# Ten result slots a head, gates on GpSimd and measured spacings in the attention; disjoint scatter views and another order in the experts

## The chip, the core and the metric

The kernel runs on one core of a Trainium2 chip. The metric is the time of one execution on the device in microseconds (us), the median of several runs. The engines are named as the profile does: PE (TensorE, matrix products; PEld are its weight loads), DVE (VectorE), ACT (ScalarE), POOL (GpSimd) and SP (SyncE, which issues most DMAs). SBUF is the on-chip memory; PSUM is the accumulator memory that PE writes, in banks of 2 KB per partition.

## The reference

The input is a causal attention over 8 batches x 8 heads x 576 positions x 64 columns, mixed with a linear memory, followed by a mixture of 8 experts that each take 576 of the 4608 tokens.

```python
a = softmax(causal(q @ k.T / 8)); local = a @ v
phi = where(q > 0, q, exp(q) - 1) + 1
mem = (phi @ M_prev) / (phi @ z_prev + 1e-6)
g = sigmoid(beta); x = g * mem + (1 - g) * local      # 4608 x 512
logits = x @ w_gate                                   # 4608 x 8
# tokens go to experts by descending logit, each expert takes at most 576
out[mask_e] = relu(x[mask_e] @ w1[e]) @ w2[e]         # 512 -> 1024 -> 512
```

## The kernel before

All tensors that go into PE are split into two half-precision parts (`h`/`l`: high and low), so a product is two or three matrix products. The program is written by a list scheduler that runs when the kernel is built (`class Sched`): each operation is added with the engines that may run it, modelled durations, the buffers that it acquires and releases, and a priority; `run` puts them into one fixed order per engine. The engines then run in that order and wait on each other by semaphores. The tables `PR` (attention) and `PM` (experts) hold the numbers that set priorities and choices.

The attention has 16 units, each one batch and half of its heads (4 heads). Per unit: loads of k, q, v (`kf`, `qf`, `vf`); the cast to the high half (`h`, line 1076) and the low half (`h<-kf,h`, line 1166); PE transposes with copies out of PSUM (`kT`, `qT`, `pT`, lines 1175 and 1076); `maxes`, the row maxima (`mx`, line 1189; `mfin`, line 1238, joins the last two columns); phi in three steps into `ef`: Relu of -q on ACT (line 1258), Exp on ACT in SBUF (line 1259), and max(q, 0) + that on DVE (line 1260, both inputs in SBUF); and per head three score blocks on PE into one of five `pb` banks, their exponentials on ACT (`ph`, `pf`) and the low halves on DVE (line 1328) or POOL (line 1331).

Then `outs` makes the results of a head in PSUM (`avs`). Five 65-column slots (64 values and a denominator) for the softmax part are in one of two banks. The five for the memory part are in a third bank that both share. On PE, AV1, AV2, AV3 (softmax part) come first and AVm (memory part) after them. On DVE, N0 (line 1370) makes the ten scaled denominators `de`, N1 (line 1371) their reciprocals, N2 (line 1378) multiplies the five softmax slots into `xt` and frees their bank, and N3 (line 1381) adds the memory part in five instructions of 64 columns and frees the shared bank. One head in four goes another way: N2 (line 1375) writes all ten products, and POOL adds the halves. `xt` is split into `xs`, transposed and stored, and the gate logits are made from it.

At the start `put` (lines 1134 to 1137, for two buffers) writes the gate 1 - g and its low half into columns of `V`, on DVE.

The second part (`moe_all`): per expert, twelve rounds find the threshold (`scs` on ACT, line 1752, `scr` on DVE, line 1754, and a small product `pr` on PE), lists of tokens are made, POOL gathers the rows (line 1597), DMAs transpose them, and `ffn` runs both layers on PE (`ph`, `prem`, `py`, line 1520), the hidden values being split on ACT (`hh`) and DVE (`hl`). The weights come in as `wst`, are cast to `wh` on ACT, and their low halves `wl` are made on POOL (line 1670). The second layer goes over five row tiles, four of 128 rows and one of 64 (i = 4), in the order 0 to 4; each tile's result is scattered by POOL into `out` (line 1732). A scatter waits for the one before it (`chain('scat')`). Expert n+1's routing runs under expert n's products.

Of the kernel before, what the change touches and what calls it, by code (L numbers as in the profile page):

```python
# [8 lines left out]
F32 = mybir.dt.float32  # L9
# [14 lines left out]
          'kba': 26167.38,  # L24
          'kbd': 89934.43,
          'kbv': -42750.78,
          'kha': -31764.59,
          'khp': 5106.93,
          'khv': 15537.51,
          'klp': -38678.8,  # L30
          'klv': -12296.22,
          'mh2a': -17575.07,
          'mh2v': -38018.38,
          'mha': -30814.97,
          'mhv': 34437.85,
          'mlp': -26689.75,
          'mlv': 38649.36,
          'mra': -9141.16,
          'mrv': -19840.62,
          'mza': 26263.38,  # L40
          'mzv': 45776.8,
          'nap': -923.34,
          'nav': -3267.9,
          'nca': -15205.18,
          'ncp': 5726.56,
          'ncv': -19200.53,
          'nsp': -44039.97,
          'nsv': 53036.19,
          'p2p': 3448.83,
          'p2v': -5.41,  # L50
          'p4sp': -13138.26,
          'p4sv': 4463.41,
          'pha': 62090.66,
          'php': 8056.32,
          'phra': -11781.08,
          'phrv': 36271.85,
          'phv': -18601.34,
          'plp': 4268.08,
          'plv': 4386.98,
          'prepca': -16428.03,  # L60
          'prepcv': -61075.56,
          'qha': -54438.84,
          'qhp': 68999.41,
          'qhv': 27006.28,
          'qlp': -35173.26,
          'qlv': 35145.28,
          'qmovea': 40086.94,
          'qmoved': 6923.88,
          'qmovev': -23898.79,
          'tea': -3548.59,  # L70
          'tev': -3860.39,
          'vha': 17808.76,
          'vhp': -32370.21,
          'vhv': 12384.67,
          'vlp': 7100.74,
          'vlv': 7492.31,
          'xtea': -60996.71,
          'xtev': 65701.69},
 'dl': {'0': {'AV': 229.41,
              'MX': -299.44,  # L80
              'N': -122.24,
              'P2': -238.25,
              'S': -181.67,
              'fin1': -583.08,
              'fin2': 161.03,
              'kb': -80.89,
              'kh': -512.02,
              'kl': -358.78,
              'kt': -439.53,
              'lk': -419.49,  # L90
              'lm': -165.74,
              'lq': -302.48,
              'lv': -171.69,
              'maxrem': -221.35,
              'mfin': 51.89,
              'mfin2': -464.52,
              'mfin3': -610.95,
              'mh': -444.19,
              'ml': -76.83,
              'mz': -143.61,  # L100
              'nadd': -366.59,
              'ncast': 128.52,
              'nsub': -549.22,
              'ph': 175.87,
              'phe': -855.14,
              'phr': -231.1,
              'phs': -8.28,
              'pl': -296.83,
              'prep': -367.83,
              'proc24': 185.7,  # L110
              'pt': -154.32,
              'qh': -277.87,
              'ql': 222.21,
              'qmove': -115.3,
              'qt': -209.49,
              'sj4': -498.53,
              'vh': -32.95,
              'vl': 422.02},
        '1': {'AV': 141.02,
              'MX': -120.86,  # L120
              'N': -19.99,
              'P2': -148.77,
              'S': 605.64,
              'fin1': 364.35,
              'fin2': -284.85,
              'kb': -201.95,
              'kh': -238.36,
              'kl': 4.99,
              'kt': -141.23,
              'lk': -251.21,  # L130
              'lm': -135.14,
              'lq': -176.42,
              'lv': -139.99,
              'maxrem': 172.04,
              'mfin': -280.96,
              'mfin2': 436.53,
              'mfin3': -88.16,
              'mh': -255.82,
              'ml': 444.23,
              'mz': 664.47,  # L140
              'nadd': -199.3,
              'ncast': -335.9,
              'nsub': 425.14,
              'ph': -361.93,
              'phe': -211.15,
              'phr': -422.34,
              'phs': -83.34,
              'pl': 189.38,
              'prep': -86.64,
              'proc24': 489.9,  # L150
              'pt': 44.01,
              'qh': -488.06,
              'ql': 808.27,
              'qmove': 469.27,
              'qt': 58.07,
              'sj4': 36.09,
              'vh': 211.96,
              'vl': -368.71},
        '10': {'AV': 202.31,
               'N': -70.03,  # L160
               'P2': 42.34,
               'S': -8.78,
               'fin1': 257.07,
               'fin2': 104.54,
               'kb': 430.3,
# [853 lines left out]
def attention(ctx,tc,q,k,v,M_prev,z_prev,beta,wg,xd,L1,NB,cst,rcst):  # L1019
    nc=tc.nc  # L1020
# [850 lines left out]
```

## Time and profile before

| what | value |
|---|---|
| median of 3 runs (lowest, highest) | 977.39 us (977.2, 980.42) |
| the profiled execution's own time | 981.21 us |
| its span in the trace | 979.4 us |
| PE busy in the span | 811.6 us (83%) |
| DVE busy | 727.3 us (74%) |
| ACT busy | 602.5 us (62%) |
| POOL busy | 581.8 us (59%) |

The span is the time from the first to the last recorded event; the run's time is 1.8 us longer. Busy shares are means over the span; the stages differ, so the stretches must be read one by one. The attention runs from 0 to about 500 us, the first expert's routing to about 561 us, the experts' products to about 970 us.

### The profile page before, as it was taken

What the parts mean: (1) busy time and instruction counts of PE and PEld (TensorE: products, weight loads), DVE (VectorE), ACT (ScalarE), POOL (GpSimd) and SP (SyncE); (2) the same over time, 40 slices, a digit from 0 to 9 for tenths busy, and PEclk for the clock granted to TensorE, in tenths of its full rate; (3) what the DMA queues carried; (4) which work ended last, traced back from release to release, by engine and by line L of the source; (5) the groups of instructions that cost most, each with busy time, mean ns of one, the idle gap of its engine ahead of it and who ended that gap; (6) DMA issues with size and microseconds to landing.
All of it is one profiled execution on the core that took longest, in us unless ns stands there. A gap on an engine that the chain in (4) does not pass through costs nothing.

```text
span 979.4 us, 25245 instructions
## 1 busy us (share of the span) xinstructions
PE 811.6 (83%) x9736; PEld 523.0 (53%) x9736; DVE 727.3 (74%) x2374; ACT 602.5 (62%) x1047; POOL 581.8 (59%) x560
## 2 busy tenths in 40 slices
PE   4487777887887988888841697999999999999995
PEld 2375665666776767766630543445444444444442
DVE  8999888888989998897668977768777777602010
ACT  4397857869788787777712557383748383754110
POOL 6586876788689895877710237382646464595101
PEclk8699988999999998999955699899999999999998
DMA  6466455454675542633411417362727273692101
GB/s 133 87 141 136 100 114 117 115 126 90 142 140 115 113 95 56 137 69 66 83 47 40 182 73 224 110 185 76 231 75 246 83 246 96 224 265 94 38 12 38
DMA packets 230302, 116.49 MB, mean 119 GB/s; under 512 B 199013, under 2 KB 208229, under 8 KB 230181
## 3 DMA queue, kind: packets, MB, share of 16 engines
q1 hardware_dynamic: 224293, 96.00, 39.1%
q0 software_dynamic: 5888, 18.88, 5.8%
q8 instruction: 76, 1.25, 0.5%
q14 instruction: 45, 0.37, 0.1%
HBM read 72.40 MB, written 18.87 MB: 93 GB/s over the span
## 4 chain that ended last, share of the span: by engine, by line
PE 56%; DVE 25%; issue 5%; POOL 5%; ACT 4%; SPq 2%; DMA 2%; DVEq 0%; POOLq 0%; ACTq 0%
PE py L1520 19%; PE ph L1520 17%; PE avs L1033 8%; PE pb L1033 6%; DVE xt L1381 4%; DVE mx L1189 4%; DVE pl L1328 3%; PE prem L1520 2%; DVE scr L1754 2%; PE pb L1175 2%; DVE xt L1378 2%; SPq L1093 2%; DVE ef L1260 1%; PE pr L1520 1%; POOL V L1275 1%
## 5 line engine op out<-in xcount | busy, mean ns | idle before, releaser
L1670 POOL TENSOR_TENSOR wl<-wst,wh 128x1024 f16<-128x1024 f32 x60 | 127.6, 2149 | 84.6 <-ACT wh L1669 66.5
L1520 PE MATMUL ph<-xT,wh 128*128 128x512 f16 (+1 forms) x560 | 164.3, 367 | 1.4 <-DVE hl L1713 0.7
L1323 ACT ACTIVATE ph<-pb 128x512 f16<-128x512 f32 x192 | 115.1, 600 | 40.4 <-PE pb L1033 24.9
L1189 DVE TENSOR_REDUCE mx<-pb 128x1 f32<-128x512 f32 (+5 forms) x273 | 130.4, 527 | 6.0 <-PE pb L1033 3.6
L1033 PE MATMUL avs<-V,ph 128*128 128x65 f16 x1792 | 104.7, 196 | 32.1 <-DVE xt L1381 20.4
L1033 PEld LDWEIGHTS <-ph 128*128 128x128 f16 x1792 | 95.8, 100 | 42.0 <-issue 39.1
L1331 POOL TENSOR_TENSOR pl<-pf,ph 128x512 f16<-128x512 f32 x80 | 96.5, 1210 | 32.4 <-ACT pf L1330 25.7
L1033 PE MATMUL pb<-kT,qM 128*128 128x256 f16 (+5 forms) x384 | 86.8, 327 | 31.5 <-DVE qM L1076 13.5
L1732 POOL DMA_INDIRECT out_dram<-ys,idx x40 | 38.9, 971 | 124.7 <-ACT ys L1727 63.8
L1033 PE MATMUL pb<-qT,kT 128*128 128x64 f16 (+3 forms) x576 | 101.9, 242 | 11.1 <-DVE pl L1328 3.2
L1033 PE MATMUL avs<-V,pl 128*128 128x65 f16 x896 | 100.5, 199 | 0.0
L1520 PEld LDWEIGHTS <-wh 128*128 128x128 f16 x1072 | 68.5, 99 | 59.3 <-issue 4.2
L1520 PE MATMUL ph<-xT,wl 128*128 128x512 f16 (+1 forms) x280 | 98.8, 367 | 0.0
L1520 PE MATMUL py<-wl,hh 128*128 128x512 f16 x256 | 97.0, 379 | 0.0
L1520 PE MATMUL py<-wh,hh 128*128 128x512 f16 x256 | 97.0, 379 | 0.0
L1033 PE MATMUL pb<-qM,kB 128*128 128x64 f16 (+3 forms) x576 | 97.0, 241 | 0.0
L1520 PE MATMUL prem<-xT,wh 128*128 128x64 f16 x512 | 96.9, 194 | 0.0
L1713 DVE SCALAR_TENSOR_TENSOR hl<-ph,hh 128x512 f16<-128x512 f32 x64 | 44.0, 688 | 63.4 <-ACT hh L1712 63.1
L1752 ACT ACTIVATE scs<-p_LwT,th 128x320 f16<-128x320 f32 x84 | 47.0, 560 | 67.4 <-DVE th L1761 51.8
L1754 DVE TENSOR_SCALAR_CACHE_REDUCE scr<-p_LwT,th 128x320 f16<-128x320 f32 x168 | 85.1, 544 | 3.0 <-DVE th L1761 0.4
L1033 PEld LDWEIGHTS <-pl 128*128 128x128 f16 x896 | 86.2, 100 | 0.0
L1712 ACT ACTIVATE hh<-ph 128x512 f16<-128x512 f32 x64 | 37.9, 594 | 77.2 <-PE ph L1520 51.7
(285 smaller groups left out, 2294.6 us busy)
## 6 DMA issues: line engine op xcount, KB each, us to landing
wst<-in_moe_w_dram SPq DMA_DIRECT2D x32, 1024.0 KB
kf<-in_k_dram SPq DMA_DIRECT2D x64, 128.0 KB
qf<-in_q_dram SPq DMA_DIRECT2D x64, 128.0 KB
vf<-in_v_dram SPq DMA_DIRECT2D x64, 128.0 KB
xd<-xs SPq DMA_DIRECT2D x16, 512.0 KB
kB<-kT SPq DMA_DIRECT2D x15, 288.0 KB
kf<-in_k_dram SPq DMA_DIRECT2D x32, 32.0 KB
qf<-in_q_dram SPq DMA_DIRECT2D x32, 32.0 KB
```

What stands on the lines that cost most here:

```text
L1033: def MM(*a,**kw): mm(*a,skip_group_check=True,**kw)
L1189: R=lambda o,i: nc.vector.tensor_reduce(o,i,axis=mybir.AxisListType.X,op=ALU.max)
L1323: c=SC.add('Eh',[('A',478)],lambda x,a=a: nc.scalar.activation(phs_[x.buf['ph']][:,0:512],pbb[a.buf['pb']],AF.Exp,scale=0.125),acq=('ph',) ...
L1331: e=SC.add('P2',[('P',1113)],lambda x,c=c,d=d: nc.gpsimd.tensor_sub(pls_[c.buf['ph']][:,0:512],pfs[d.buf['pf']],phs_[c.buf['ph']][:,0:512] ...
L1381: for i in range(5): nc.vector.scalar_tensor_tensor(xt()[:,0,i],avv()[:,1-b,i,0:64],de[:,1-b,i:i+1],xt()[:,0,i],op0=ALU.mult,op1=ALU.add)
L1520: def MM(*a,**kw): mm(*a,skip_group_check=True,**kw)
L1670: SC.add('sp',[('P',2079)],lambda x,ws=ws,k=k,s=s: G_.tensor_sub(wl[:,k,s],ws(),wh[:,k,s]),r=[key+('h',)],w=[key+('l',)],after=[b],rel=rel ...
L1712: b=SC.add('hh',[('A',478)],lambda x,a0=a0,f=f: A_.activation(hh[:,f],phb[a0.buf['ph']],AF.Relu),w=[('hh',f)],after=[y],prio=pr('hh',n,pos ...
L1713: SC.add('hl',[('V',602)],lambda x,a0=a0,f=f: V_.scalar_tensor_tensor(hl[:,f],phb[a0.buf['ph']],0.0,hh[:,f],op0=ALU.max,op1=ALU.subtract), ...
L1732: z=SC.add('scat',[('P',655 if i<4 else 330,'p',0,(1034,'n'))],lambda x,e=e,i=i,r_=r_: G_.indirect_dma_start(out=out,out_offset=bass.Indir ...
L1752: SC.add('sign',[('A',547)],lambda x,j=j,t_=t_,c_=c_: A_.activation(scs[j-KV],LwT,AF.Sign,bias=t_[:,4:5],accum_out=c_[:,j:j+1]),r=['LwT',( ...
L1754: V(462,lambda x,j=j,t_=t_,c_=c_: V_.tensor_scalar(scr[j],LwT,t_[:,j+1:j+2],0.0,op0=ALU.is_ge,op1=ALU.add,accum_out=c_[:,j:j+1]),r=['LwT', ...
```

## The change

In the attention:

- A head's ten result slots are all doubled: seven are in the head's own bank (two such banks), three in a part of the shared bank (195 columns for each of the two). The pool `am` is gone. AVm now comes first, before the head's exponentials are needed, and takes the double slot; AV1 to AV3 follow.
- N0 is two instructions (seven and three columns). N2 is two products for the memory part (128 and 192 columns, into `xt`), N2b multiplies the five softmax slots in place in PSUM (320 columns), and N3 adds PSUM and `xt` in one instruction of 320 columns. Both banks' slots are freed by N3. The POOL head's N2 is two instructions (448 and 192 columns). `eps` is one tile of ten columns, written by ten small instructions instead of four.
- `put` runs on POOL instead of DVE.
- phi: the Exp writes into PSUM (`pb`) in pieces of 512, 512 and 128 columns, and the DVE step reads q from SBUF and the other input from PSUM, in the same pieces (17 DVE instructions become 48). The tables now put the Relu on DVE (15 of 128x1152), and the 15 high-half casts of q of that size, on DVE before, on POOL; 11 copies of `kT`, 3 of `pT` and 6 of `qT` move from ACT to DVE.
- The partial maxima `maxremr` are written to PSUM and read there by `mfin`. The logits are added into `Lw` directly, without copies.
- Modelled spacings of PE and of the gathers and scatters, the set of operations `LK` that the scheduler keeps apart on DVE and POOL, and all numbers of both tables are new.

In the experts:

- `outv` is a list of 40 views of `out` that are declared disjoint; each scatter writes its own and no longer waits for the one before.
- The second layer goes over the tiles in the order 0, 4, 1, 2, 3.
- Two of expert 0's four `wl` pieces that were on DVE are on POOL.

PE and SP run the same numbers of instructions as before (9736 products). The core of the diff (the tables left out but for a line):

```diff
+ 's0': 2}
-LK={'P2','kl','ql','pl','vl','phs','nadd','nsub','kb','qmove','p4s','ml','mh','sp','thu','base'}
+LK={'rc','qh','kh','vh','gt','lg4','prep','P2','kl','ql','pl','vl','nadd','nsub','kb','qmove','p4s','ml','mh','sp','thu','base'}
...
-                nc.vector.memset(V16[i][:,16:20,col:col+1],0.0)
+                nc.gpsimd.memset(V16[i][:,16:20,col:col+1],0.0)
...
-        one('put',[('V',740)],f,-154+20*i,r=['gt'],w=[('V16g',i)])
+        one('put',[('P',1150)],f,-154+20*i,r=['gt'],w=[('V16g',i)])
...
-            SC.add('phe',[('A',Ac(n))],lambda x,a=a,b_=b_,U2=U2: nc.scalar.activation(ef[U2][:,a:b_],ef[U2][:,a:b_],AF.Exp,scale=-1.0),w=K('ef',U2,a,b_),prio=pr('phe',u))
+            for a2,b2 in ([(a,b_)] if b_-a<9 else [(0,8),(8,16),(16,18)] if a==0 else [(a,a+8),(a+8,b_)]):
...
+                ex=SC.add('phe',[('A',Ac(n))],lambda x,a2=a2,b2=b2,U2=U2,pe_=pe_: nc.scalar.activation(pe_(x),ef[U2][:,a2:b2],AF.Exp,scale=-1.0),r=K('ef',U2,a2,b2),acq=('pb',),prio=pr('phe',u))
...
+                def slot(i): return avs[:,2*b,65*i:65*i+65] if i<7 else avs[:,1,65*(3*b+i-7):65*(3*b+i-6)]
...
-            a0=SC.add('AVm',[('T',284)],wg=650,fn=lambda x: avp(x,0),r=rm_,acq=('am',),after=[a3],prio=pr('AV',u,3*j+.4)); ch('A',a0)
+            a0=SC.add('AVm',[('T',300)],wg=650,fn=lambda x: avp(x,0),r=rm_,acq=('av',),after=ch('A'),prio=pr('AV',u,3*j)); box[0]=a0; ch('A',a0)
+            a1=SC.add('AV1',[('T',279)],wg=585,fn=lambda x: avp(x,1),r=rv,after=[a0]+ce,prio=pr('AV',u,3*j+.1))
...
-                    for i in range(5): nc.vector.scalar_tensor_tensor(xt()[:,0,i],avv()[:,1-b,i,0:64],de[:,1-b,i:i+1],xt()[:,0,i],op0=ALU.mult,op1=ALU.add)
...
+                def f(x): t=xts[x.buf['xt']][:,0]; MU(t[:,0:2],own(5,7)[:,:,0:64],dv(5,7)); MU(t[:,2:5],mid()[:,:,0:64],dv(7,10))
...
+                n2b=SC.add('N2b',[('V',402)],lambda x: MU(own(0,5)[:,:,0:64],own(0,5)[:,:,0:64],dv(0,5)),r=[('de',di)],after=[n1,n2],prio=pr('N',u,3*j+.25))
+                n3=SC.add('N3',[('V',402)],lambda x: nc.vector.tensor_tensor(xt()[:,0],own(0,5)[:,:,0:64],xt()[:,0],op=ALU.add),after=[n2b],rel=[('av',a0)],prio=pr('N',u,3*j+.3))
...
+    outv=dram_disjoint_views(out,40)
...
-        for i in range(5):
+        for i in (0,4,1,2,3):
...
-            z=SC.add('scat',[('P',655 if i<4 else 330,'p',0,(1034,'n'))],lambda x,e=e,i=i,r_=r_: G_.indirect_dma_start(out=out,out_offset=bass.IndirectOffsetOnAxis(ap=idx[0:r_,i:i+1],axis=0),in_=yss[e.buf['ys']][0:r_],in_offset=None),r=[('idx',n%3,i)],after=[e]+chain('scat'),rel=[('ys',e)],prio=pr('scat',n,pos[0])); chain('scat',z)
+            SC.add('scat',[('P',1250 if i<4 else 1200,'p',0,(1250,'n'))],lambda x,e=e,i=i,r_=r_: G_.indirect_dma_start(out=outv[5*n+i],out_offset=bass.IndirectOffsetOnAxis(ap=idx[0:r_,i:i+1],axis=0),in_=yss[e.buf['ys']][0:r_],in_offset=None),r=[('idx',n%3,i)],after=[e],rel=[('ys',e)],prio=pr('scat',n,pos[0]))
```

What this does to the order of instructions shows at three places. The first is the start, on DVE before: the second half of `put` (`V_102`; `gt` is the gate, `cl` its low half) stands in DVE's row directly ahead of the copies into `qT` and `qM`.

```order
50 L1135 MEMSET V_102 128x4
51 L1136 CAST V_102<-gt 64x2 x2
52 L1137 TENSOR_TENSOR cl_185<-gt,V_102 128x4
53 L1134 CAST V_102<-cl_185 128x16
54 L1135 MEMSET V_102 128x4
55 L1136 CAST V_102<-cl_185 64x2 x2
56 L1076 COPY mh_126<-mh_126 64x260
57 L1076 COPY qT_120<-pb_176 128x1024
58 L1076 COPY qM_98<-qT_119 64x512 x2
```

After, on POOL: the same instructions stand behind the low halves of the second k and around the high-half cast of the second q, ahead of the first `V`.

```order
51 L1066 CAST V_101<-cl_183 64x2 x2
52 L1007 TENSOR_SCALAR h_112<-qf_107 128x18x64
53 L1064 CAST V_102<-gt 128x16
54 L1065 MEMSET V_102 128x4
55 L1066 CAST V_102<-gt 64x2 x2
56 L1067 TENSOR_TENSOR cl_184<-gt,V_102 128x4
57 L1064 CAST V_102<-cl_184 128x16
58 L1065 MEMSET V_102 128x4
59 L1066 CAST V_102<-cl_184 64x2 x2
60 L1096 TENSOR_TENSOR h_112<-qf_107,h_112 128x8x64
61 L1096 TENSOR_TENSOR h_112<-qf_107,h_112 128x10x64
62 L1208 TENSOR_TENSOR V_101<-vf_108,V_101 128x12x64
```

So `put` has left DVE's row, and POOL has 14 more instructions ahead of the low half of the second q and of the first `V`.

The second place is DVE in the middle of the attention, where two heads' results are taken out of PSUM; before:

```order
482 L1378 TENSOR_TENSOR xt_162<-avs,de_160 128x320
483 L1381 SCALAR_TENSOR_TENSOR xt_162<-avs,de_160,xt_162 128x64 x5
484 L1328 TENSOR_TENSOR pl_139<-pb_176,ph_131 128x512
485 L1370 SCALAR_TENSOR_TENSOR de_159<-avs,eps_180 128x10
486 L1260 SCALAR_TENSOR_TENSOR ef_110<-qf_106,ef_110 128x1152
487 L1328 TENSOR_TENSOR pl_141<-pb_174,ph_133 128x512
488 L1371 RECIPROCAL de_159<-de_159 128x10
489 L1378 TENSOR_TENSOR xt_161<-avs,de_159 128x320
490 L1381 SCALAR_TENSOR_TENSOR xt_161<-avs,de_159,xt_161 128x64 x5
```

After, a like place (line 1307 and 1308 are N0, 1311 the products, 1325 the sum):

```order
313 L1307 SCALAR_TENSOR_TENSOR de_159<-avs,eps 128x7
314 L1308 SCALAR_TENSOR_TENSOR de_159<-avs,eps 128x3
315 L1312 RECIPROCAL de_159<-de_159 128x10
316 L1006 COPY qT_119<-pb_176 128x1024
317 L1311 TENSOR_TENSOR xt_163<-avs,de_159 128x128
318 L1311 TENSOR_TENSOR xt_163<-avs,de_159 128x192
319 L1006 COPY qT_119<-pb_177 128x256
320 L1311 TENSOR_TENSOR avs<-avs,de_159 128x5x64
321 L1261 TENSOR_TENSOR pl_140<-pb_173,ph_132 128x512
322 L1325 TENSOR_TENSOR xt_163<-avs,xt_163 128x320
```

A head now takes seven instructions (two of N0, N1, two of N2, N2b, N3) where it took eight (N0, N1, N2, five of N3), and copies still lie between them.

The third place is PE, at the memory part of a head (`mh`, `ml`: the memory's halves). Before it follows the head's last softmax product, and the DVE's N0 follows it:

```order
762 L1033 LDWEIGHTS p4h_150
763 L1033 MATMUL avs<-V_101,p4h_150 128x65
764 L1033 LDWEIGHTS p4l_152
765 L1033 MATMUL avs<-V_101,p4l_152 128x65
766 L1033 LDWEIGHTS pT_122
767 L1033 MATMUL avs<-mh_126,pT_122 128x65
```

After, it follows the transposes of another unit, and the head's softmax products come later in the row:

```order
836 L1105 LDWEIGHTS h_112
837 L1105 MATMUL pb_174<-idh,h_112 128x128
838 L963 LDWEIGHTS pT_122
839 L963 MATMUL avs<-mh_126,pT_122 128x65
840 L963 LDWEIGHTS pT_122
841 L963 MATMUL avs<-ml_128,pT_122 128x65
```

The memory part has moved from the end of a head's chain to its front, into a slot of its own.

## Rows read from the trace of the kernel before

**Rows 1.** Busy time by stretch: start:end, length, each engine, clock, DMA share, GB/s.
```profile
0.00:60.00 60.00, 31.38 (x329) 22.67 (x330) 54.58 (x117) 29.98 (x50) 39.63 (x66) 0.80 0.53 117
60.00:500.00 440.00, 358.28 (x6563) 290.85 (x6560) 382.15 (x1009) 335.08 (x588) 335.64 (x353) 0.96 0.50 106
...
600.00:620.00 20.00, 14.28 (x69) 6.01 (x67) 13.25 (x64) 14.26 (x28) 18.16 (x12) 0.74 0.53 138
620.00:970.00 350.00, 347.13 (x2280) 167.85 (x2278) 193.68 (x789) 177.93 (x293) 164.78 (x113) 1.00 0.44 140
```

**Rows 2.** Timeline of PE after its longest wait: start, length, instruction, idle before.
```profile
39.27 0.61 PE L1033 MATMUL pb<-kT,qM 128*128 128x512 f16 x1 [11.28 <-DVE qM L1076]
```

**Rows 3.** Timeline of DVE, first and last gate instruction and what follows.
```profile
26.04 0.19 DVE L1134 CAST V<-gt 128x16 f16<-128x16 f32 x1
...
28.21 0.20 DVE L1134 CAST V<-cl 128x16 f16<-128x16 f32 x1
...
34.02 1.25 DVE L1134 CAST V<-cl 128x16 f16<-128x16 f32 x1
...
35.31 2.60 DVE L1136 CAST V<-cl 64x2 f16<-64x2 f32 x2
...
38.92 0.29 DVE L1076 COPY qM<-qT 64x512 f16<-64x512 f16 x1
```

**Rows 4.** Waits of PE from 60 to 500 us: total, times, longest.
```profile
PE avs L1033 <- DVE xt L1381: 26.2, 31, 1.7
...
PE avs L1033 <- DVE xt L1378: 6.2, 9, 2.8
PE avs L1033 <- DVE xt L1375: 4.5, 7, 1.2
```

**Rows 5.** Waits of DVE from 60 to 500 us.
```profile
DVE de L1370 <- PE avs L1033: 25.1, 26, 2.8
DVE xt L1381 <- PE avs L1033: 7.1, 11, 1.1
DVE xt L1378 <- PE avs L1033: 2.9, 6, 1.0
...
DVE xt L1375 <- PE avs L1033: 2.3, 5, 0.7
```

**Rows 6.** DVE by line and shape, 0 to 500 us: busy, mean of one, idle before.
```profile
L1328 DVE TENSOR_TENSOR pl<-pb,ph 128x512 f16<-128x512 f32 x112 | 75.4, 678 | 1.2 <-ACT pb L1327 0.8
...
L1381 DVE SCALAR_TENSOR_TENSOR xt<-avs,de,xt 128x64 f32<-128x64 f32 x240 | 50.3, 276 | 7.9 <-PE avs L1033 7.1
...
L1260 DVE SCALAR_TENSOR_TENSOR ef<-qf,ef 128x1152 f32<-128x1152 f32 x15 | 27.9, 1863 | 0.0
L1378 DVE TENSOR_TENSOR xt<-avs,de 128x320 f32<-128x320 f32 x48 | 23.4, 487 | 6.4 <-PE avs L1033 2.9 <-issue 1.0 <-POOL ml L1266 0.5
...
L1076 DVE CAST h<-qf 128x1152 f16<-128x1152 f32 x15 | 13.7, 913 | 1.5 <-DMA qf<-in_q_dram 1.4
...
L1375 DVE TENSOR_TENSOR xt<-avs,de 128x640 f32<-128x640 f32 x16 | 13.2, 822 | 3.2 <-PE avs L1033 2.3
L1076 DVE COPY kT<-pb 128x1024 f16<-128x1024 f16 x19 | 12.7, 679 | 1.1 <-PE pb L1175 1.0
L1370 DVE SCALAR_TENSOR_TENSOR de<-avs,eps 128x10 f32<-128x10 f32 x64 | 10.4, 163 | 25.4 <-PE avs L1033 25.1
...
L1238 DVE TENSOR_TENSOR mx<-mx 128x2 f32<-128x2 f32 x15 | 7.6, 511 | 0.0
```

**Rows 7.** GpSimd (POOL), the same view: a cast of 1280 columns.
```profile
L1077 POOL TENSOR_SCALAR V<-vf 128x1280 f16<-128x1280 f32 x15 | 19.3, 1288 | 9.8 <-PE avs L1033 9.8
```

**Rows 8.** Waits of PE from 600 to 620 us.
```profile
PE pr L1520 <- ACT scs L1752: 4.3, 3, 2.3
PE pr L1520 <- DVE scr L1754: 1.4, 1, 1.4
```

**Rows 9.** GpSimd by line from 500 us to the end: the weight pieces.
```profile
L1670 POOL TENSOR_TENSOR wl<-wst,wh 128x1024 f16<-128x1024 f32 x60 | 127.6, 2149 | 84.6 <-ACT wh L1669 66.5 <-issue 16.5 <-POOL wl L1670 1.3
```

More of the change, by code (lines that the diff above doesn't have):

```diff
@@ L5 @@
 import concourse.tile as tile
+from concourse.ap import dram_disjoint_views
 from concourse import mybir
@@ L41 @@
-          'mzv': 45776.8,
+          'kba': -30628.42,
+          'kbd': -21514.39,
+          'kbv': -30457.33,
+          'kha': -9689.05,
+          'khp': 68039.52,
+          'khv': 14252.18,
+          'klp': -32138.21,
+          'klv': -19015.13,
+          'mh2a': 18046.34,
+          'mh2v': -7557.72,
+          'mha': -6556.62,
+          'mhv': 118047.29,
+          'mlp': -61301.72,
+          'mlv': 103205.55,
+          'mra': 13094.26,
+          'mrv': -49929.19,
+          'mza': 13667.92,
@@ new lines @@
+          'p4sp': -99613.75,
+          'p4sv': -14317.61,
+          'pha': -24715.3,
+          'php': 10489.25,
+          'phra': -10695.76,
+          'phrv': 20287.52,
+          'phv': -24278.1,
+          'plp': 4297.99,
+          'plv': 4879.76,
+          'prepca': -46562.05,
+          'prepcv': -134550.89,
+          'qha': -51241.95,
+          'qhp': 17974.64,
+          'qhv': -60171.16,
+          'qlp': 26287.18,
+          'qlv': 78420.0,
+          'qmovea': 42586.74,
+          'qmoved': 5914.55,
@@ L755 @@
  'p2k': 'vpvpvvpvpvpv',
[L756 to L758 removed]
+ 'pin': {'kb': 'd*va',
+         'kh': '*',
+         'kl': '*pp',
          'mh': '*',
          'mh2': 'a',
[L761 removed]
+         'ml': 'p',
          'mr': 'a',
@@ L1355, in avp @@
                             w,c=col(i,j); bi=B_[w][0].buf['ph']; ph,pl=phs_[bi][:,c:c+128],pls_[bi][:,c:c+128]
-                        o=avs[:,2*(x if part==1 else box[0]).buf['av'],65*i:65*i+65]
+                        o=slot(i)
                         MM(o,ph,vv[:,65:130],start=j==0,stop=False)
@@ new lines, in outs @@
+            a1=SC.add('AV1',[('T',279)],wg=585,fn=lambda x: avp(x,1),r=rv,after=[a0]+ce,prio=pr('AV',u,3*j+.1))
+            a2=SC.add('AV2',[('T',647)],wg=1365,fn=lambda x: avp(x,2),r=rv,after=[a1],prio=pr('AV',u,3*j+.2))
+            a3=SC.add('AV3',[('T',465)],wg=877,fn=lambda x: avp(x,3),r=rv+[('p4l',U2,x) for x in range(h2,2)]+[('p4h',U2,x) for x in range(h2,2)],after=[a2],rel=[('ph',c) for c,e in B_],prio=pr('AV',u,3*j+.3))
+            bi=lambda: a0.buf['av']
+            own=lambda a,b: avs[:,2*bi(),65*a:65*b].rearrange('p (i e) -> p i e',e=65)
@@ new lines, in outs, with f @@
+            mid=lambda: avs[:,1,195*bi():195*bi()+195].rearrange('p (i e) -> p i e',e=65)
+            di=(4*u+j)%2; de=des[di].rearrange('p k i -> p (k i)'); eg=lambda a,b: eps[:,g,a:b]
+            def f(x):
+                nc.vector.scalar_tensor_tensor(de[:,0:7],own(0,7)[:,:,64],1.0/256,eg(0,7),op0=ALU.mult,op1=ALU.add)
+                nc.vector.scalar_tensor_tensor(de[:,7:10],mid()[:,:,64],1.0/256,eg(7,10),op0=ALU.mult,op1=ALU.add)
+            n0=SC.add('N0',[('V',158)],f,r=['gt'],w=[('de',di)],after=[a3],prio=pr('N',u,3*j))
```

1617 lines of the change are left out of this document (751 added, 866 removed).

## The prediction

> **What bounds the kernel now.** I read the busy time by stretch first [rows 1]. There are three regimes. From 0 to 60 us DVE is busy for 54.58 of 60 us and PE for 31.38. From 60 to 500 us, the body of the attention, DVE is busy for 382.15 of 440 us and PE for 358.28: no engine is full, DVE is the fullest, 57.9 us of it are idle. From 620 to 970 us PE is busy for 347.13 of 350 us at full clock: there is nothing to gain there but by taking products away, and the change takes none. Between them, from 600 to 620 us, PE is busy for only 14.28 us and its granted clock is 0.74. So three stretches can give time: the start, the body of the attention, and the step from expert 0 to expert 1.
>
> The waits say what holds each. In the start the timeline of PE has one hole of 11.28 us, which ends at 39.27 us with a copy into qM on DVE [rows 2]. DVE is not idle then: its timeline [rows 3] has `put` from 26.04 to 37.91 us (14 instructions, and two others among them), then the copies that PE waits for, at 38.92. In the body PE waits for DVE to empty `avs`, 26.2 + 6.2 + 4.5 = 36.9 us in three rows [rows 4], and DVE waits for PE to fill `avs`, 25.1 + 7.1 + 2.9 + 2.3 = 37.4 us in four [rows 5]. That is a ping-pong over one shared bank: PE can't write a head's memory part before N3 of the head ahead has read the bank, and DVE's N0 can't start before that memory part is there.
>
> **The start.** `put` leaves DVE: 37.91 - 26.04 = 11.9 us, of which I take 11 for the 14 instructions, on the path, since PE's hole ends right behind it. What takes its place ahead of the copies is not free. The order puts phi's new pieces, an additional Relu and more copies ahead of DVE's first N0, some 7 us by the prices below, of which 4 to 5 are work for later units and only drawn forward. Gain: at most 11, at least 11 - 7 = 4; I take **7**. POOL takes `put`; it was busy for 39.63 of the first 60 us [rows 1], so 20 us of room cover it if each takes as long there as on DVE (11). If the first `V` came late by it, PE's first `avs` would be late: that is the lower end.
>
> A cast of 128x16 took 0.20 us at 28.21 and 1.25 us at 34.02 [rows 3]; the same instruction, six times the time, so most of `put` is not work but waiting for something. The Trainium skill, page "SBUF — State Buffer", section "Who interferes with whom", says that DVE and GpSimd share a pair of ports, held by one instruction until it ends, and that a DVE copy or cast can need it. The trace agrees as far as these two rows go. By that rule `put` on POOL would cost less than the 11 us that I allow, and the new Relus on DVE could suffer the same: the fourth rival.
>
> **The body of the attention, what DVE has to do.** Priced from the groups by line and shape [rows 6]:
> - N0: 64 more at 163 ns: +10.4.
> - N1 stays. N2 and N3: before 50.3 + 23.4 + 13.2 = 86.9 us. A product of 320 columns takes 487 ns, one of 640 columns 822 ns, so 1.05 ns a column; 128, 192 and 448 columns come to 0.29, 0.35 and 0.62 us. After, for 48 heads: 48 x (0.29 + 0.35 + 2 x 0.487) = 77.5, for 16 heads 16 x (0.62 + 0.35) = 15.5; together 93.0, so +6.1. No row shows an instruction of DVE that writes PSUM. I take 0.487 for N2b, the row of the same size; the upper bound is 5 x 0.21 = 1.05 us, what five pieces take (50.3/240 each): +27 for the 48.
> - 20 copies from ACT: 11 of kT at 0.68 = 7.5, 9 of the smaller groups, some +3.5: +11.
> - phi: 1.863 for 128x1152 with both inputs in SBUF. With one input in PSUM, 128x512 takes 0.678 (the row of line 1328), so 2 x 0.678 + 0.29 = 1.65; 15 x -0.22 = -3.3.
> - mfin: 511 ns for two columns in SBUF; with PSUM in it I take N0's 163: -5.2. The bounds are 0 and that.
> - Relu for cast, 15 each of 128x1152: 913 ns for the cast; the Relu has twice the bytes to write. I count 0, bound +5 by 1.3 times the cast.
>
> The sum is **+19** us of DVE (about +14 to +46 with the bounds). It speaks against the change, since DVE is the fullest engine here. POOL gains some 19 (15 casts at 1.29, the row of 1280 columns [rows 7]) on 335.64 of 440, still 85 us free; ACT only loses work.
>
> **The body, what the second slot gives.** With all slots doubled and the memory part first, PE fills head h+1 while DVE empties head h; none of the waits in [rows 4, 5] has its cause any more. If all of DVE's 37.4 us go, the body takes 382.15 + 19 busy + (57.9 - 37.4 = 20.5) other idle = 422 us instead of 440: -18. If half go, 440: 0. What is late next is DVE itself: PE then waits for its copies (kT, qT, pl) instead of for `avs`, and the five `pb` banks, which now also hold phi's Exp, are one more thing to wait for. I take a value between, **-10**: 78% of DVE's waits gone.
>
> **The first routing and the step to expert 1.** Expert 0's two `wl` pieces that pass to POOL stand between its gathers; one takes 2.15 us [rows 9], so the fifth gather is later by that at most, and DVE has two fewer in the same stretch: between 0 and +2.5, I take **+1**. From 600 to 620 us PE lost 20 - 14.28 = 5.7 us to waiting, and after the waits it ran its products at half clock: the granted clock is 0.74 in the stretch and 1.00 from 620 on [rows 1]. Of the waits 4.3 are on `scs` and 1.4 on `scr` [rows 8], that is on expert 1's routing rounds which are late, behind which its token lists and gathers come. A product in the half-clock part takes twice as long, some 4 more; about 9.5 us are at stake. After, the lists' indices are computed one pair of reductions earlier, and expert 0's second layer has its short tile second, so that more products lie over the gathers. That moves the step by 2 to 3 us, not by all of it; and if PE's hole is shorter the clock need not fall. I take **-4**; bounds 0 and -9.5.
>
> The scatters' wait for the one before lies on POOL, off PE's path: PE is busy for 347 of 350 us with it. Disjoint views give nothing in that stretch. The order of tiles changes which tile's copies end the kernel, by less than 1 us; I count 0.
>
> **Sum.** -7 - 10 + 1 - 4 = -20 against the profiled execution's own time of 981.21 us: 961.2. That execution is 0.4% over the median (977.39 / 981.21 = 0.9961): **957 us**.
>
> **The rivals**, each on the profiled time and then times 0.9961:
> - *The waits in the body only move* (22%). Both sides wait 37 us, but DVE gets 19 more; 57.9 - 19 leaves 39 idle, as after any engine that is nearly full. Body 0: 981.2 - 7 + 1 - 4 = 971.2, **967**. For it: DVE is at 87% there.
> - *All of it comes back* (12%): body -18, start -11, step -9.5, routing 0: 942.7, **939**. For it: the holes in [rows 2, 4] have one cause each, and the change removes it. Against: +19 on DVE.
> - *DVE's new instructions decide* (9%), the other side. The waits were only DVE's lateness, so every added microsecond from 60 to 500 us is paid: +19, at the in-place product's upper price +46. With -7 + 1 - 4 that is 990 to 1017, **986** at the low price. It decides from a body that is longer by 15 us on: -10 + 15 = +5 is 0.5% slower. That is 0.23 us for each of 64 heads, so N2b or N3 need be only a little dearer than 0.487.
> - *DVE and POOL get in each other's way more* (9%). The short cast at 34.02 lost 1.05 us to a POOL instruction beside it; 15 Relus on DVE and 15 large casts of 1.29 us on POOL, each with one such loss, are 30 x 1.05 = 32 at worst, 16 by half. Body -10 + 16 = +6: 981.2 - 7 + 6 + 1 - 4 = 977.2, **973**, not to be told from no change.
>
> The remaining 48% are for the sum. **Range:** 940 to 974 us; it leaves out the slower case, half of the fourth and a little of the best one. A measurement of this kernel tells about 0.5% from no change, that is 972.5 to 982.3. Faster: the sum, the best case and most of the first rival, 0.81; the same 0.11; slower 0.08.
>
> **What would show it.** In the profile after: `put` on POOL, and PE's longest hole ahead of 60 us no longer 11 us; in the body PE's waits for `avs` under 10 us, DVE busy for about 400 us of some 430, and its waits for `avs` near 8 us; N2b and N3 at 0.49 us, phi's pieces at 0.68; PE's busy time in 20 us around expert 1's first products nearer to 18, with the clock at 1.00; the experts' stretch as long as before. The prediction is wrong if N2b is far dearer than 0.49, if PE now waits on `pb` for DVE's copies as long as it did for `avs`, if the first `V` on POOL opens a new hole in the start, or if the step to expert 1 keeps its hole.

## The result and the profile after

The changed kernel takes 985.86 us (median of 4 runs, 983.65 to 987.18) against 978.24 us for the kernel before: 1.0077 times as long, with a 95% interval of 1.0055 to 1.0099. It is slower, by 0.8%. A second set of runs, on another chip, gave 983.49 us and 1.0074 [1.0046, 1.0103]. The profiled execution took 987.18 us with a span of 985.4 us, 6.0 us more than before.

The busy time by stretch, which answers to [rows 1]:

```profile
0.00:60.00 60.00, 35.25 (x402) 25.72 (x403) 53.99 (x124) 31.47 (x59) 48.23 (x88) 0.94 0.57 125
60.00:500.00 440.00, 361.37 (x6522) 290.57 (x6520) 378.45 (x1017) 309.97 (x580) 344.80 (x366) 0.96 0.49 106
600.00:620.00 20.00, 19.59 (x124) 9.23 (x123) 16.05 (x78) 13.13 (x30) 14.84 (x10) 1.00 0.49 110
620.00:970.00 350.00, 340.74 (x2225) 163.52 (x2224) 189.91 (x776) 173.94 (x289) 165.35 (x112) 1.00 0.47 139
```

The step to expert 1, from 600 to 620 us, is repaired: PE is busy for 19.59 us instead of 14.28, at full clock. But from 620 to 970 us it is now busy for 340.74 us instead of 347.13. To find where the time goes I took two fixed points on PE: the transpose of `p_big`, with which the first routing begins, and expert 0's first product over full rows. Here they are in the timeline of PE, of before:

```profile
505.46 0.48 PE L1514 MATMUL pb<-identf,p_big 64*64 64x64 f32 x4 [2.43 <-DVE p_big L1443]
...
561.49 0.38 PE L1520 MATMUL ph<-xT,wh 128*128 128x512 f16 x1 [0.71 <-DVE hl L1713]
```

and of after:

```profile
502.14 0.48 PE L1456 MATMUL pb<-identf,p_big 64*64 64x64 f32 x4 [2.27 <-DVE p_big L1385]
...
563.14 0.38 PE L1462 MATMUL ph<-xT,wh 128*128 128x512 f16 x1 [0.96 <-DVE hl L1657]
```

In this trace the attention ends 3.3 us earlier. From there to the first full product it takes 61.0 us instead of 56.0, a loss of 5.0. The rest of the span, 985.4 - 563.14 = 422.3 against 979.4 - 561.49 = 417.9, loses 4.4. Together: -3.3 + 5.0 + 4.4 = +6, the difference of the spans.

The first surprise is in the attention. The waits that the ten slots should have taken away are all there, PE's [rows 4] and DVE's [rows 5]; the waits from 60 to 500 us after (total, times, longest), first PE's:

```profile
PE avs L963 <- DVE xt L1311: 16.6, 29, 1.9
...
PE avs L963 <- DVE xt L1325: 9.7, 14, 2.3
PE avs L963 <- DVE avs L1311: 9.4, 15, 1.8
...
PE avs L963 <- DVE de L1308: 3.3, 9, 0.8
```

and DVE's:

```profile
DVE avs L1311 <- PE avs L963: 14.4, 19, 1.8
DVE de L1307 <- PE avs L963: 9.9, 16, 1.3
DVE xt L1311 <- PE avs L963: 9.3, 17, 1.8
DVE xt L1325 <- PE avs L963: 7.9, 13, 1.0
```

PE waits for 39.0 us in these four rows where it waited for 36.9, DVE for 41.5 where it was 37.4. The reader should look at the third DVE row and the first: N2 and the in-place product wait for PE, though the N0 ahead of them has already waited for the last product of their own head. They can only be waiting for the next head, which PE writes into the other slot. One such place, in DVE's timeline:

```profile
102.36 0.55 DVE L1311 TENSOR_TENSOR xt<-avs,de 128x128 f32<-128x128 f32 x2
...
104.08 0.50 DVE L1311 TENSOR_TENSOR avs<-avs,de 128x320 f32<-128x320 f32 x1 [0.58 <-PE avs L963]
```

and in PE's:

```profile
102.96 0.22 PE L963 MATMUL avs<-V,ph 128*128 128x65 f16 x2 [0.66 <-DVE xt L1311]
...
104.63 0.22 PE L963 MATMUL avs<-V,ph 128*128 128x65 f16 x2 [0.59 <-DVE avs L1311]
```

The head that DVE empties here was complete when its N0 ran, at 100.76 us, so PE's products from 102.96 on belong to the next one. They start when DVE's two products end; DVE's in-place product starts when PE pauses; PE goes on when that product has ended. In the records of the trace, 25 of the 48 in-place products carry a wait on PE of their own. The reading that the experiments test: `avs` is one tile of three banks, and an access to it is made to wait for an earlier one by the other engine, whichever bank that was in. In the kernel before the softmax banks would then wait for each other in the same way.

The second surprise is in the experts. At expert 7 the timeline of POOL has one row for its weight pieces:

```profile
833.69 14.63 POOL L1614 TENSOR_TENSOR wl<-wst,wh 128x1024 f16<-128x1024 f32 x7
```

DVE's has beside it:

```profile
840.03 0.69 DVE L1657 SCALAR_TENSOR_TENSOR hl<-ph,hh 128x512 f16<-128x512 f32 x1 [1.41 <-ACT hh L1656]
840.64 0.15 DVE L1538 TENSOR_SCALAR tk<-pl 128x5 f32<-128x5 f32 x1
840.83 7.52 DVE L1538 TENSOR_TENSOR idx<-tk,pp 128x5 int32<-128x5 f32 x1
848.27 1.28 DVE L1657 SCALAR_TENSOR_TENSOR hl<-ph,hh 128x512 f16<-128x512 f32 x2
```

and PE's behind it:

```profile
849.00 0.59 PE L1462 MATMUL ph<-xT,wh 128*128 128x512 f16 x1 [3.73 <-DVE hl L1657]
```

An addition of five columns takes 7.52 us instead of 0.16, and ends at 848.35, when POOL's seven weight pieces end (833.69 + 14.63 = 848.32). Two `hl` behind it on DVE are late, PE waits 3.73 us and then runs at half clock (0.59 us for the product instead of 0.38). The `hl` at 840.03, with 512 columns and an input from PSUM, took its usual 0.69 us in the middle of the same seven pieces. The additions for expert 0's gathers lie beside the moved pieces in the same way, one of DVE's and the piece on POOL beside it:

```profile
542.87 1.82 DVE L1538 TENSOR_TENSOR idx<-tk,pp 128x1 int32<-128x1 f32 x1
```

and

```profile
542.56 2.12 POOL L1614 TENSOR_TENSOR wl<-wst,wh 128x1024 f16<-128x1024 f32 x1 [0.77 <-issue]
```

Again both end together, at 544.7.

In the start PE's hole of 11.28 us [rows 2] is gone. `put` takes 3.8 us on POOL (two times nine instructions between 20.86 and 25.80 us, 1.9 us each time) where it took 11.9 on DVE; the pair of casts that took 2.60 us there [rows 3] is the last of it, in POOL's timeline:

```profile
25.38 0.42 POOL L1066 CAST V<-cl 64x2 f16<-64x2 f32 x2
25.87 2.51 POOL L1096 TENSOR_TENSOR h<-qf,h 128x512 f16<-128x512 f32 x2
28.34 2.59 POOL L1208 TENSOR_TENSOR V<-vf,V 128x768 f16<-128x768 f32 x2
30.89 1.29 POOL L1007 TENSOR_SCALAR V<-vf 128x1280 f16<-128x1280 f32 x1
32.14 0.67 POOL L1199 TENSOR_TENSOR ml<-mf,mh 64x260 f16<-64x260 f32 x1
32.78 2.58 POOL L1208 TENSOR_TENSOR V<-vf,V 128x512 f16<-128x512 f32 x2
```

But a new hole has come, of 6.55 us, in PE's timeline:

```profile
36.67 0.37 PE L1171 MATMUL pb<-identf,mx 128*1 128x128 f32 x1 [6.55 <-DVE mx L1168]
```

Its reason stands in DVE's, at three instructions of 32 columns for the gate weights:

```profile
29.90 1.06 DVE L1074 TENSOR_SCALAR wf<-wf 128x32 f32<-128x32 f32 x1
31.00 1.22 DVE L1074 CAST wgs<-wf 128x32 f16<-128x32 f32 x1
32.25 3.16 DVE L1074 TENSOR_TENSOR wgs<-wf,wgs 128x32 f16<-128x32 f32 x1
```

They end at 30.96, 32.22 and 35.41 us, and pieces on POOL end at 30.93, 32.18 and 35.36. In the kernel before, where POOL stood idle when they ran (39.45 to 40.07 us), each took 0.18 to 0.19 us. The third has both inputs in SBUF and ends with the third POOL instruction from where it began (`ml` and two on `V`), two of which began after it.

The prices of single DVE instructions came out as taken, but for the Relu of line 1188 (by line and shape, 0 to 505 us):

```profile
L1311 DVE TENSOR_TENSOR avs<-avs,de 128x320 f32<-128x320 f32 x48 | 23.8, 496 | 15.0 <-PE avs L963 14.4
L1325 DVE TENSOR_TENSOR xt<-avs,xt 128x320 f32<-128x320 f32 x48 | 23.4, 487 | 8.8 <-PE avs L963 7.9
...
L1193 DVE SCALAR_TENSOR_TENSOR ef<-qf,pb 128x512 f32<-128x512 f32 x32 | 21.5, 670 | 0.9 <-ACT pb L1192 0.8
...
L1188 DVE TENSOR_SCALAR ef<-qf 128x1152 f32<-128x1152 f32 x15 | 17.6, 1173 | 0.3 <-POOL p L1096 0.3
...
L1168 DVE TENSOR_TENSOR mx<-mx,pb 128x2 f32<-128x2 f32 x15 | 2.1, 150 | 0.1
```

### The profile page after: what moved, and what is told of

It is laid out like the page before. It is cut to its first block, busy times and chain, and to the rows that moved or that the text cites. A ratio compares the mean times of both kernels' runs of the same rounds, so it can differ in the third digit from the quotient of the medians.

```text
span 985.4 us, 25314 instructions
## 1 busy us (share of the span) xinstructions
PE 817.6 (83%) x9736; PEld 523.0 (53%) x9736; DVE 720.6 (73%) x2383; ACT 578.4 (59%) x1048; POOL 605.2 (61%) x596
## 4 chain that ended last, share of the span: by engine, by line
PE 32%; issue 9%; DVE 9%; ACT 1%; POOL 1%; DMA 1%; another core or an unknown queue 0%; POOLq 0%; DVEq 0%; SPq 0%; ACTq 0%
PE py L1462 14%; PE ph L1462 11%; PE avs L963 3%; DVE scr L1698 2%; PE prem L1462 1%; DVE idx L1538 1%; PE pr L1462 1%; POOL out_dram L1676 1%; PE pb L963 1%; DVE xt L1311 1%; DMA xg<-xd,idx 1%; DMA wst<-in_moe_w_dram 1%; DVE th L1705 0%; DVE avs L1311 0%; ACT wst L1612 0%
## 5 line engine op out<-in xcount | busy, mean ns | idle before, releaser
L1614 POOL TENSOR_TENSOR wl<-wst,wh 128x1024 f16<-128x1024 f32 x62 | 132.6, 2158 | 94.2 <-ACT wh L1613 66.4
L1119 DVE TENSOR_REDUCE mx<-pb 128x1 f32<-128x512 f32 (+3 forms) x256 | 123.4, 547 | 3.1 <-PE pb L963 2.1
L963 PE MATMUL pb<-kT,qM 128*128 128x256 f16 (+5 forms) x384 | 84.7, 317 | 16.6 <-DVE mx L1119 9.6
L1261 DVE TENSOR_TENSOR pl<-pb,ph 128x512 f16<-128x512 f32 x112 | 76.0, 681 | 4.6 <-ACT pb L1260 3.8
```

The source lines that it names most:

```text
L963: def MM(*a,**kw): mm(*a,skip_group_check=True,**kw)
L1119: R=lambda o,i: nc.vector.tensor_reduce(o,i,axis=mybir.AxisListType.X,op=ALU.max)
L1261: e=SC.add('P2v',[('V',602)],lambda x,a=a,c=c: nc.vector.tensor_sub(pls_[c.buf['ph']][:,0:512],pbb[a.buf['pb']],phs_[c.buf['ph']][:,0:512] ...
L1614: SC.add('sp',[('P',2079)],lambda x,ws=ws,k=k,s=s: G_.tensor_sub(wl[:,k,s],ws(),wh[:,k,s]),r=[key+('h',)],w=[key+('l',)],after=[b],rel=rel ...
```

## The experiments

All are compared with the kernel before, run on the same chip. The theory after the first look at the traces: the attention gained nothing much because `avs` is one tile, and the experts lost because additions on DVE with both inputs in SBUF wait behind POOL. The rivals were that DVE is full (the attention), and that the new order of the experts is slow by itself.

**Halves of the change.** The experts' function, its table and the set `LK` for it are taken from before, the attention from after.

> The attention of after with the experts of before. Reading of the two traces: the gate to the first routing round comes 3.3 us earlier after the change (503.98 for 507.30 us), and everything lost is lost behind it. If that holds, this kernel is 3 us faster than before: ratio 0.996 to 0.998, about 975 us. Rival: the attention's end leaves the experts worse off (weights, stores, buffers later), and the loss goes with the attention: ratio 1.003 or more.

Measured: 972.78 us, 0.995 [0.9919, 0.9981]. The attention part of the change is faster than before, by some 5 us; the experts' part costs the difference to 1.0074, about 12 us, though the trace after shows only 9.4 behind the attention; this half's own first routing begins at 497.88 us, 4 us earlier than after's with the same attention. Six traces hold this attention with the one tile (after, after once more, and the edits of its experts). They begin the first routing between 497.55 and 502.14 us, 3.3 to 7.9 us ahead of before. Between the two ends, after and the run with the order of row tiles, PE's idle time from 60 us to its first product on `p_big` (498.46 and 493.88 us) is the same, 78.4 and 78.5 us; its busy time is 360.1 and 355.4 us, at a granted clock of 0.96 and 0.98. So that spread lies in PE's pace, with its clock, and not in the waits; why the clock differed stays open.

**Three tiles instead of one.** Only the tile is split. In the kernel after, the instructions and their order stay; in the kernel before, the denominators and the product of 640 columns become two instructions each. The core of the edit on the kernel after:

```diff
-    avs=ps.tile([128,3,512],F32,name='avs')
+    avt=[ps.tile([128,512],F32,name=f'avs{i}') for i in range(3)]
...
-            own=lambda a,b: avs[:,2*bi(),65*a:65*b].rearrange('p (i e) -> p i e',e=65)
+            own=lambda a,b: avt[2*bi()][:,65*a:65*b].rearrange('p (i e) -> p i e',e=65)
```

> After, with the results in three PSUM tiles of one bank each in place of one tile of three banks; the instructions and their order are the same. Theory A: the waits on avs that stayed after the change (39 us of PE, 42 us of DVE) are put in because both slots lie in one tile, though the accesses are in different banks; without them the attention ends 8 to 20 us earlier, about 970 us, ratio to before 0.985 to 0.998. Rival B: DVE is full, the waits are its lateness and move to pb: less than 3 us, ratio to before 1.005 or more.

> Before, with the results in three PSUM tiles of one bank each; the denominators and the POOL head's product are then two instructions instead of one (64 and 16 more, some 10 + 3 us of DVE). Theory A: 37 us of PE's waits on avs in the body are mostly for accesses to another bank; 10 to 20 us go, 13 us of DVE work come, ratio 0.985 to 1.0. Rival: the third bank, shared by both heads, is what PE waits for (one slot for the memory part), as the prediction had it; the tiles change nothing and the 13 us count: ratio 1.0 to 1.013.

Measured: after with three tiles 949.28 us, 0.9697 [0.9642, 0.9753]; before with three tiles 952.65 us, 0.9724 [0.9668, 0.9779]. Both gain more than any theory gave: the split takes 3.8% off the kernel after (0.9697 for 1.0077) and 2.8% off the kernel before. The waits on `avs`, of after with three tiles, from 60 to 460 us, PE's:

```profile
PE avs L963 <- DVE xt L1325: 4.9, 6, 2.2
...
PE avs L963 <- DVE xt L1311: 3.5, 6, 1.1
```

and DVE's:

```profile
DVE de L1307 <- PE avs L963: 3.9, 9, 1.0
```

Two smaller rows of DVE add 0.9 and 0.8 us, and none of the 48 in-place products carries a wait on PE of its own any more. In before with three tiles, where the memory part still has a single slot, PE waits 10.8 us for DVE to empty `avs` (from 60 to 475 us; 8.4 in the two rows above) and DVE 5.2 us for PE to fill it.

The fixed points on PE, of after with three tiles, and of before with three tiles:

```profile
463.90 0.48 PE L1456 MATMUL pb<-identf,p_big 64*64 64x64 f32 x4 [2.26 <-DVE p_big L1385]
```

and

```profile
477.39 0.48 PE L1514 MATMUL pb<-identf,p_big 64*64 64x64 f32 x4 [2.43 <-DVE p_big L1443]
```

No instruction was taken away and no buffer added, and the attention ends 38 us earlier than in the kernel after, and 28 us earlier than in the kernel before. That settles it: most of the waits stood between accesses that touch different banks, and DVE was not full, since it does the same work in 38 us less. With that gone, the change's whole attention, with `put` and the tables, is worth 477.39 - 463.90 = 13.5 us (12.4 to 15.6 in the six traces that have it on three tiles); with the one tile, 3.3 to 7.9.

**The weight pieces.** All four of expert 0's first low pieces are on DVE again (`'s0': 4`, the default).

> After, with all four of expert 0's first low weight pieces on DVE again, as before, none of them on POOL between the gathers. In the trace after, two index additions on DVE lie beside these POOL pieces and take 1.82 and 1.29 us instead of 0.16, and the last gather is late. Theory: 3 to 5 us come back, about 982 us, ratio to before 1.002 to 1.005. Rival: the gathers are late for another reason (the order of the list's instructions), DVE has 2.4 us more to do, and nothing comes back: ratio 1.007 or more.

Measured: 979.02 us, 0.9993 [0.9966, 1.0021]. Some 7 us come back, more than expected, and they don't come from the first routing alone: to the first full product it takes 59.85 us (501.95 to 561.80) instead of 61.0. The scheduler ordered the experts anew, and expert 7's addition then took 3.91 us instead of 7.52.

**The attention of after with three tiles, the experts of before.**

> The attention of after with the three tiles, and the experts of before. If the terms add (attention of after -5 us as measured, tiles -36 us on after, experts as before), 937 us, ratio 0.955 to 0.965. Against before with three tiles (952.65 us) it then shows what the ten slots give once the waits are per bank: 12 to 18 us. Rival: the experts take some of it back, as a shorter attention leaves less time for the first weights: ratio over 0.968.

Measured: 937.68 us, 0.9607 [0.9583, 0.9631], as the sum of the terms had it. Against before with three tiles (0.9724) the ten slots and the rest of the attention's edits, `put` among them, give 1.2%, a little under the 12 to 18 us expected. What the slots give by themselves no run shows.

**The index in one instruction.**

```diff
-V_.tensor_scalar(tks[:,a:b],e[:,a:b,1],-64.0,None,op0=ALU.mult); V_.tensor_tensor(idx[:,a:b],tks[:,a:b],pps[:,a:b],op=ALU.add)
+V_.scalar_tensor_tensor(idx[:,a:b],e[:,a:b,1],-64.0,pps[:,a:b],op0=ALU.mult,op1=ALU.add)
```

> After, with the row index of the gathers computed in one DVE instruction that reads the token number from PSUM and the position from SBUF, in place of two, the second with both inputs in SBUF. Theory: that addition waits while POOL runs weight pieces back to back (7.52 us for 5 columns at 840.83 in the trace after, 1.82 and 1.29 in the first routing), because the two engines share a way into SBUF that an input from PSUM doesn't need. Then the one instruction takes under 0.3 us everywhere, PE's hole of 3.73 us near 845 goes, and 4 to 9 us come back: 977 to 982 us, ratio to before 0.999 to 1.004. Rival: the wait is something else (a semaphore or the queue of DVE), the single instruction is as long: ratio 1.006 or more.

Measured: 968.21 us, 0.9936 [0.9914, 0.9957]. It is faster than before. The instructions of the line in this kernel (minimum, median and maximum in ns):

```profile
L1538 DVE SCALAR_TENSOR_TENSOR idx<-pl,pp x12: 143/158/165, 534.9 to 825.8; 128x5 int32<-128x5 f32 x7, 128x1 int32<-128x1 f32 x5
```

None waits any more, whatever POOL does. The gain, 1.4%, is larger than the stalls of the trace. PE's waits at expert 1 to 7 (657, 756, 783, 793, 849 us after, 7.9 us together) are gone too, but only the last follows from an addition directly. The others can't be put down to the additions: after with three tiles and this same edit, below, has the same order of the experts and no long addition either, and PE's waits for `scr` and `scs` are still there (4.0 us, for 4.2 in after). Why they go in this kernel stays open.

**`put` on DVE again**, as in before, in the kernel after.

> After, with the gates written by DVE again; the scheduler orders anew. Theory of the prediction: put lies on the path in the start, on POOL it is nearly free, so this kernel is 4 to 8 us slower than after: ratio to before 1.011 to 1.017. Rival: the start is bound by something that put only hides (loads, POOL's low halves), nothing changes: ratio 1.005 to 1.010.

Measured: 995.67 us, 1.0199 [1.0172, 1.0225], 1.2% over after. The first routing begins at 516.58 us instead of 502.14, so the loss is larger than the theory's. But it is not the price of `put`. The scheduler's new order put all of `put` where POOL stood idle (32.61 to 37.16 us), and there it takes 2.8 us on DVE, from 34.46 to the end of this row:

```profile
36.91 0.35 DVE L1066 CAST V<-cl 64x2 f16<-64x2 f32 x2
```

What became slow are the ten instructions for `eps`, which now lie beside four subtractions on POOL (21.40 to 26.47 us); in the kernel after they took 0.86 us. DVE's row, and PE's behind it:

```profile
21.73 4.99 DVE L1058 TENSOR_SCALAR eps<-gt 128x8 f32<-128x8 f32 x10
```

and

```profile
27.36 1.25 PE L963 MATMUL pb<-kT,qM 128*64 128x512 f16 x3 [4.86 <-DVE mx L1119]
```

In the first 60 us the granted clock is 0.82 here and 0.94 in after. How the 14.4 us divide among `eps`, `put`, the clock and the rest of the new order is not shown.

**The order of the row tiles** 0 to 4 in the kernel after.

> After, with the second layer's row tiles in the order 0, 1, 2, 3, 4 again; the scheduler orders anew. 13 us of the loss lie in the experts (972.78 for 985.86 us), of which the weight pieces account for about 7. Theory: the short tile second makes the hidden values' low halves late (PE waits 1.51 us for hh at 588 and 0.41 for ys at 602 us); order 0 to 4 gives back 2 to 6 us: ratio 1.002 to 1.006. Rival: the order costs nothing, the rest is the stalled index additions: ratio 1.007 or more, or a changed order that moves the stalls elsewhere.

Measured: 973.6 us, 0.9983 [0.9965, 1.0001]: more than the theory gave. But the trace has expert 7's addition at 1.17 us in this kernel, not 7.52, since the scheduler's order differs. So this run does not price the order itself.

**Controls and the sums.**

> After once more, unchanged, beside the others on one chip: 982 to 990 us by its first runs, ratio 1.004 to 1.011. If it came out as fast as the kernels with one edit (968 to 979 us), what those gained would have been the chip and not the edit.

Measured: 983.49 us, 1.0074 [1.0046, 1.0103]. The gains above are not the chip's.

> Before, with the row index computed in one instruction with an input from PSUM. In the trace before, the index additions lose 1.14, 0.68, 0.83 and 0.79 us beside POOL's weight pieces, and expert 1's gathers come right behind the first of these. Theory: 1 to 5 us come back, ratio 0.995 to 0.999. Rival: before, POOL's pieces stand so that no addition is on the path: ratio 0.998 to 1.002.

Measured: 977.18 us, 0.9997 [0.998, 1.0015]. The rival holds: the same additions wait before the change, but for 0.7 to 1.1 us and nowhere on the path. The weak place was there; the change's order put it in the way.

> After with both edits, three tiles and the index in one instruction. If the two causes are independent: 985.9 - 36 - 17 = 933 us, ratio 0.952 to 0.960. Rival: a part of each is the same loss, or the stalls move to other instructions: ratio over 0.962.

Measured: 942.69 us, 0.9646 [0.9619, 0.9674]. The two are not independent: on three tiles the index gives 0.5%, within the intervals, not 1.4%. In the trace of after with three tiles POOL and DVE meet otherwise: expert 7's addition takes 0.48 us there.

> The attention of after with three tiles, the experts of before, and the index in one instruction. With what the index gives on before (1 to 5 us) 933 to 937 us, ratio 0.955 to 0.960. Against the kernel with the experts of after and the same two edits it shows what the change's own expert part is worth when the stalls are gone: by the prediction 3 us in its favour, by the first experiments 3 to 6 us against it.

Measured: 937.64 us, 0.9602 [0.9576, 0.9627]. This, the kernel without the index edit and the last kernel below are the fastest of all, 4% under before. The experts of before beat those of after by 5 us even without stalled additions.

> The attention of after with three tiles, the experts of before, the index in one instruction (937.64 us), with the disjoint views and without the chain of scatters. Theory of the prediction: the scatters' waits lie on POOL, off PE's path, nothing changes: 0 to 1 us, ratio 0.958 to 0.961. Rival: without the chain POOL's row has scatters elsewhere, between the weight pieces and gathers, and the next expert is late: 3 to 5 us slower, ratio 0.963 or more.

> The same kernel with the row tiles in the order 0, 4, 1, 2, 3 and nothing else. Theory: PE now comes to the short tile, which needs hr and its low half, earlier, and then to tile 1 while its input is read; after it PE waits (1.51 us for hh at 588 us and 0.41 for ys at 602 us in the trace after) once in expert 0: 1 to 3 us slower, ratio 0.961 to 0.964. Rival: the order moves the last tile's two copies off the end and gives 1 us: ratio 0.958 to 0.960.

Measured, both on one chip: with the views 940.56 us, 0.9649 [0.9621, 0.9678]; with the order 937.83 us, 0.9619 [0.96, 0.9639]. The order costs nothing that can be seen. The views without the chain have a ratio where their rival had it (0.963 or more), and are 0.3% slower than the order's run, with intervals that overlap: they bring nothing, and may cost some. What remains of the 5 us must lie with the moved weight pieces, the modelled spacings, the set `LK` and the table's numbers; it stays open.

## Why the prediction was wrong

The forecast was 957 us, from 940 to 974; measured were 985.86. The profile after has +6 us where the sum had -20: the attention gave 3.3 us (up to 7.9 in other traces of it) where start and body were to give 17, the first routing cost 5.0 for 1, and behind it 4.4 were lost where 4 were to be won.

**What bounds the kernel** was read rightly: the start and the step to expert 1 moved with the change, and the body with the split of the tile.

**The start** was forecast at -7. PE's busy time in the first 60 us rose by 3.9 us, at a granted clock of 0.94 instead of 0.80. That `put` was dear on DVE through waiting and cheap on POOL holds: 11.9 us became 3.8, where 11 were allowed. But that it was dear came from POOL's work beside it, not from DVE: its last two casts in before ended at 37.91 us, POOL's two pieces beside them at 37.89, and with POOL idle all of it takes 2.8 us on DVE. What takes its place is not copies, as the step had it, but DVE's `wgs`, which now waits for POOL in its turn.

**The body, what the second slot gives** (-10): this step failed. It says that "none of the waits in [rows 4, 5] has its cause any more", because PE could not write a head's memory part before the shared bank had been read. The rows show who waits for whom, not for which bank; I took the bank that the code's pools named. The waits were on the tile, and 39.0 us of PE's and 41.5 of DVE's stayed. The shared bank was a small part of them: with three tiles a single slot for the memory part leaves 10.8 us of PE's waits on `avs` and two leave 8.4, a difference of 2.4. That the whole attention is worth 13.5 us on three tiles does not make the -10 right: it holds the start, for which another 7 were forecast, and all other edits.

**The body, what DVE has to do** (+19) was mis-sized, though not by its prices: the in-place product took 496 ns (487 taken), phi's pieces 670 (678), mfin 150 (163); only the Relu was dearer, 1173 ns, 3.9 us over the casts. Up to the first routing DVE's busy time fell from 440.11 to 434.31 us; without `put` (10.9 us) and the three instructions for the gate weights (0.6 us before, 5.4 after) it did not change. The slip is in one term: the records of neighbours on DVE overlap. The five pieces of N3 were put down at the time that they fill together (240 in 50.3 us), and the new instructions at their full durations. At its full duration, 276 ns, the old group is 66.2 us, and the sum comes to +3 instead of +19.

**The first routing** (+1) and **the step to expert 1** (-4): the step was repaired as forecast, by 5.3 us of PE's busy time between 600 and 620 us. The order of the row tiles is not enough for that: put into the experts of before by itself, it leaves 4.0 us of PE's waits for `scs` there, for 5.4 without it. The routing cost 5.0. I had priced the piece between the gathers by its own 2.15 us, and left out what it does to DVE beside it. That is a part: with the index in one instruction the first routing takes 58.3 us (498.36 to 556.67) instead of 61.0, with the pieces back on DVE 59.85; with the experts of before it takes 56.0 (497.88 to 553.88). The rest of the 5.0 comes with the new order of the experts, and its cause is open. The experts behind it lost to slow additions too, of which the forecast had nothing, but not to them alone: with no slow addition on either side the experts of before are still 5 us ahead.

On the body, the first rival, in which the waits only move (22%), had the nearest number, 0, but not the reason: it had DVE nearly full.

Of the rivals, the one in which DVE and POOL get in each other's way was the nearest in kind, with 9%, and in the wrong place: it was looked for in the Relus of the attention, and struck the gate weights and additions of one to five columns. The Trainium skill, page "SBUF — State Buffer", section "Who interferes with whom", states that a DVE instruction with two SBUF inputs contends with a GpSimd instruction that reads SBUF, and that one with at most one SBUF input outside the two-port modes does not. The runs agree: with one of the two inputs in PSUM the longest addition takes 0.165 us instead of 7.52. They add that such an instruction can wait for several POOL instructions in a row and not for one only.

## What to carry to other kernels

Before pricing a second buffer, look at what the waits are between: if the two halves of a double buffer lie in one tile, the wait may stay, and splitting the tile by banks was worth 2.8% on the kernel before and 3.8% on the kernel after. A small instruction on VectorE whose inputs are both in SBUF can cost as much as the train of GpSimd work beside it, whatever its columns; here casts and scalar operations from SBUF to SBUF did so too (`put`, `wgs`, `eps`). Take one input from PSUM, or keep it apart. When adding up instructions, count both sides in the same way, by full durations or by the time that they fill. A run in which the scheduler orders anew prices the new order, and not the edit alone. An edit whose worth depends on where two engines meet has to be tried on the version that will be kept: the same index edit gave nothing, 0.5% or 1.4%.

## What was not expected of the hardware

An addition of 128x5 waited on VectorE for 7.4 us while GpSimd ran seven 128x1024 subtractions back to back, of which at least three began after it had begun to wait (seven in 14.63 us, 2.09 each). In the same stretch an instruction of 512 columns with an input from PSUM was not held up at all.
